# Sliding-window attention and two MoE layers: maxima over partitions on TensorE, lower halves and squares on GpSimd, a new instruction order

## The chip, the cores and the metric

The kernel runs on one core of a Trainium2 chip. The metric is the device time of one execution in microseconds (us), median of the runs; smaller is better. TensorE is called PE, VectorE DVE, ScalarE ACT, GpSimd POOL and SyncE, which issues the DMAs, SP.

## What is computed

The reference, cut to what matters (4 batches, 8 heads, 576 positions, head dimension 64, window 64; d_model 512, d_ff 1536):

```
scores = where(mask, scale * q @ k.T, -1e9);  attn = softmax(scores);  x = attn @ v     # x: 2304 tokens x 512
xn = x / sqrt(mean(x * x) + 1e-6) * rms_g
x = (silu(xn @ w_gate) * (xn @ w_val)) @ w_out                                      # first MoE layer
out = (sigmoid(x @ w_gate2) * (x @ w_val2)) @ w_out2                                # second
```

Weights arrive as float64, and the products are made as three products of f16 halves (upper by upper, upper by lower, lower by upper).

## The kernel before

The 2304 tokens are six blocks of 384. For each weight tile of the first layer (128 x 1024 values, tiles 0 to 11 alternately gate and value, 12 to 17 output) there are these steps: `w_load` (an SP DMA of 1 MB), `w_max` (maximum of the raw words on DVE, L244, then over the partitions on GpSimd, L247, then scales on DVE, L248, L249, L253, L255), `w_conv` (ACT L271, DVE L272 and L273: f64 words to f32), and `w_split` (upper half on ACT, L337, lower half on DVE, L339).

The attention works in pairs of pieces of 64 queries: `st_s` makes scores on PE (mask product L400, scores L406) and reduces them (L413 to L416, L418), ACT takes exponentials (L422), DVE sums and normalises (L423, L424, L431 or ACT L429); `st_tr` transposes on PE (L439), `st_pv` multiplies with the values (L476), copies (L478) and squares (ACT L481). `rms_first` takes the mean of the squares by a PE product (L519, L521), a power on GpSimd (L522), spreads the result over the partitions by PE (L527, L528) and scales x (L531); `split_first` makes its f16 halves (ACT L536, DVE L537). These must be done ahead of the first MoE product.

A gate unit of the first MoE layer is 12 products for the gate (`moe_g`, L576, into one of two PSUM banks, tag "gv"), ACT tanh L588, DVE L589, 12 products for the value (`moe_v`, L576 too), DVE L599, then the halves of h (`moe_h`, ACT L609 and DVE L610). There are 12 such units per block. The output product of a block is `moe_o` (L625 to L627). Blocks 2 to 5 and the second layer use other forms (L782, L893).

The order of instructions on every engine comes from one table of numbers, ORDER, which `arrange` turns into dependencies between neighbours of an engine. So a row of the order lists below stands where the table puts it, and engines meet only at their waits.

## Time and profile before

| | us |
|---|---|
| median of 3 runs (869.39, 869.86, 869.9) | 869.86 |
| profiled execution | 868.72 |
| its span | 866.9 |
| PE busy in the span | 844.9 |
| DVE busy | 728.7 |
| ACT busy | 552.8 |
| GpSimd busy | 36.5 |

The span is what the trace covers, from the first instruction to the end of the last output transfer; 1.8 us of the profiled execution lie outside. Its own time is 1.1 us under the median of the runs. Busy time is summed over instructions of an engine; the share alone doesn't say which one sets the end.

### The profile page before, as it was taken

To read this page: it belongs to the slowest core of one execution; us is meant where nothing else is said; L and a number is where in the kernel's file an instruction comes from. 1 tells how busy PE (TensorE), PEld (TensorE's weight loads), DVE (VectorE), ACT (ScalarE), POOL (GpSimd) and SP (SyncE) were. 2 spreads that over 40 slices of the span, in tenths; PEclk is the share of its full clock that TensorE was granted. 3 is DMA by queue.
4 is the path that set the end of the run, shared out by engine and by line. 5 is a ranking of instruction groups with operands and counts; after the bars stand their busy time and mean duration, and the time that the engine had idled before them with its cause. 6 is when DMAs were issued, how large, how long until landed. Compare 5 with 4: busy or idle time off the path is not lost.

```text
span 866.9 us, 15579 instructions
## 1 busy us (share of the span) xinstructions
PE 844.9 (97%) x6084; PEld 522.0 (60%) x6084; DVE 728.7 (84%) x1387; ACT 552.8 (64%) x1214; POOL 36.5 (4%) x46
## 2 busy tenths in 40 slices
PE   4799999999999999999999999999999999999998
PEld 3566666666666666666666666666666666666664
DVE  6999999989887796979789889999979859535695
ACT  5988878766568776355565567677557567235541
POOL 0100200100000100100000000000000000000000
PEclk8799999999999999999999999999999999999999
DMA  9764433121202035202412766446151112024034
GB/s 341 281 219 180 179 159 99 43 94 48 87 31 81 1 141 189 79 1 86 158 50 98 231 225 231 156 149 228 53 170 50 49 44 87 1 82 146 1 110 155
DMA packets 33193, 104.19 MB, mean 120 GB/s; under 512 B 3808, under 2 KB 11360, under 8 KB 27872
## 3 DMA queue, kind: packets, MB, share of 16 engines
q1 hardware_dynamic: 33120, 103.20, 34.0%
q8 instruction: 47, 0.77, 0.4%
q14 instruction: 26, 0.21, 0.1%
HBM read 82.35 MB, written 20.84 MB: 119 GB/s over the span
## 4 chain that ended last, share of the span: by engine, by line
PE 82%; DVE 12%; ACT 2%; DMA 2%; issue 1%; SPq 1%; POOL 0%; ACTq 0%; DVEq 0%
PE bank L782 46%; PE bank L893 14%; PE bank L576 5%; PE bank L625 4%; PE bank L626 4%; PE bank L627 4%; DVE wl L339 2%; DMA wl<-in_moe_w_gate_dram 2%; DVE wl L273 1%; PE bank L476 1%; PE bank L439 1%; PE bank L406 1%; ACT sm L422 1%; DVE th L599 1%; DVE wmax L244 1%
## 5 line engine op out<-in xcount | busy, mean ns | idle before, releaser
L782 PEld LDWEIGHTS <-wl 128*128 128x128 f16 x2520 | 245.9, 98 | 163.5 <-issue 1.5
L782 PE MATMUL bank<-att,wl 128*128 128x384 f16 x2016 | 338.1, 326 | 0.0
L893 PEld LDWEIGHTS <-wl 128*128 128x128 f16 x756 | 74.0, 98 | 48.9
L576 PE MATMUL bank<-xhl,wl 128*128 128x384 f16 x576 | 98.4, 326 | 0.1
L795 ACT ACTIVATE bank<-bank 128x384 f32<-128x384 f32 x120 | 56.5, 475 | 62.0 <-PE bank L782 31.9
L782 PE MATMUL bank<-xhl,wl 128*128 128x384 f16 x504 | 86.5, 326 | 0.2 <-ACT bank L795 0.2
L576 PEld LDWEIGHTS <-wl 128*128 128x128 f16 x576 | 55.5, 98 | 36.4 <-issue 0.7
L625 PE MATMUL bank<-wl,wl 128*128 128x384 f16 x192 | 62.7, 326 | 0.2
L627 PE MATMUL bank<-wl,wl 128*128 128x384 f16 x192 | 62.6, 326 | 0.0
L626 PE MATMUL bank<-wl,wl 128*128 128x384 f16 x192 | 62.6, 326 | 0.0
L337 ACT ACTIVATE wl<-wl,isc 128x1024 f16<-128x1024 f32 (+1 forms) x48 | 54.7, 1145 | 10.2 <-DVE wl L317 4.4
L893 PE MATMUL bank<-xhl,wl 128*128 128x384 f16 x264 | 51.7, 326 | 0.0
L244 DVE TENSOR_REDUCE wmax<-wl 128x1 f32<-128x1024 f32 x36 | 43.7, 1214 | 4.7 <-DMA wl<-in_moe_w_val_dram 2.6
L422 ACT ACTIVATE sm<-sm,nm 128x128 f32<-128x128 f32 x96 | 37.2, 389 | 14.3 <-DVE nm L416 14.0
L893 PE MATMUL bank<-wl 128*128 128x384 f16 x222 | 45.9, 326 | 0.0
L271 ACT ACTIVATE wl<-wl 128x1024 f32<-128x1024 f32 x36 | 41.6, 1154 | 6.7 <-DMA wl<-in_moe_w_out_dram 3.2
L429 ACT ACTIVATE sm<-sm,su 128x128 f32<-128x128 f32 x120 | 38.6, 391 | 7.6 <-DVE su L424 7.3
L339 DVE SCALAR_TENSOR_TENSOR wl<-wl,isc,wl 128x1024 f16<-128x1024 f32 (+1 forms) x32 | 38.4, 1199 | 3.0 <-ACT wl L337 3.0
L627 PEld LDWEIGHTS <-wl 128*128 128x128 f16 x288 | 28.2, 98 | 19.1 <-issue 0.4
L625 PEld LDWEIGHTS <-wl 128*128 128x128 f16 x288 | 28.2, 98 | 18.3 <-issue 0.9
L626 PEld LDWEIGHTS <-wl 128*128 128x128 f16 x288 | 28.2, 98 | 17.8 <-issue 0.6
L247 POOL PARTITION_ALL_REDUCE amax<-wmax x30 | 17.3, 594 | 436.4 <-DVE wmax L244 404.4
(387 smaller groups left out, 1461.0 us busy)
## 6 DMA issues: line engine op xcount, KB each, us to landing
wl<-in_moe_w_out_dram SPq DMA_DIRECT2D x15, 1024.0 KB, 5.3
wl<-in_moe_w_val_dram SPq DMA_DIRECT2D x13, 1024.0 KB, 5.8
wl<-in_moe_w_gate_dram SPq DMA_DIRECT2D x13, 1024.0 KB, 5.3
att<-f SPq DMA_DIRECT2D x28, 384.0 KB, 3.8
vn<-in_v_dram SPq DMA_DIRECT2D x27, 256.0 KB, 4.2
f<-xhl SPq DMA_DIRECT2D x14, 384.0 KB, 3.9
att<-in_k_dram SPq DMA_DIRECT2D x13, 384.0 KB, 3.3
xhl<-x SPq DMA_DIRECT2D x6, 768.0 KB, 7.2
```

The source lines that it names most:

```text
L244: V.tensor_reduce(out=r1[:, i:i + 1], in_=wraw(layer, j + i)[:, :, 1].bitcast(F32), axis=AX.X, op=ALU.max, apply_absolute_value=True)
L271: A.activation(out=y.bitcast(F32), in_=hi.bitcast(F32), func=AF.Prelu, scale=2.0 ** -112, alpha=-2.0 ** 32)
L337: A.activation(out=hi, in_=y, func=AF.Copy, scale=sc)
L339: V.scalar_tensor_tensor(out=lo, in0=y, scalar=sc, in1=hi, op0=ALU.mult, op1=ALU.subtract)
L422: A.activation(out=s[e][:, c], in_=pv[e][:, c, :] if st else s[e][:, c], func=AF.Exp, scale=scale if st else 1.0, bias=nm[:, j:j + 1], acc ...
L576: T.matmul(pb[:, 0:n], lhsT=w_, rhs=x_, start=(c == 0), stop=(c == m - 1))
L625: T.matmul(o[c][:, 0:n], lhsT=wh[:, cs], rhs=hi, start=st, stop=False)
L626: T.matmul(o[c][:, 0:n], lhsT=wh[:, cs], rhs=lo, start=False, stop=False)
L627: T.matmul(o[c][:, 0:n], lhsT=wl[:, cs], rhs=hi, start=False, stop=en)
L782: T.matmul(pb[:, 0:NMAX], lhsT=w_, rhs=x[:, t, kk], start=first and kk == n == 0, stop=kk == 1 and n == 2, skip_group_check=not first)
L795: A.activation(out=o[:, 0:NMAX], in_=i[:, 0:NMAX], func=AF.Copy)
L893: T.matmul(pb[:, 0:NMAX], lhsT=w_, rhs=x[:, t], start=st and s == ss[0] and n == 0, stop=s == ss[-1] and n == 2, skip_group_check=not st)
```

## The change

Three parts of the code change, and the table of the order is new.

- `all_max` is new. It replaces the maximum over partitions on GpSimd for the first twelve weight tiles (six pairs) and for the gains: a PE transpose into a PSUM bank (L239), a small DVE reduce (L241), and a second PE transpose which spreads the result over the partitions (L242). Seven sets of three instructions.
- GpSimd takes the halves of tiles 3, 5, 7, 9 and 11 (`POOL_LO`): it scales the tile in place (L349), ACT copies the upper half (L350), GpSimd subtracts for the lower one (L352). For the other tiles the lines are L354 (ACT) and L356 (DVE). It also takes the squares of the first two pieces (L499) and the lower halves of h of block 0 (L630).
- The maxima of the second pair of weight tiles (2 and 3) are taken with those of the first, in the attention's stages, and the second conversion uses them.

```diff
@@ -42,6 +42,7 @@
          (("W", 1, 2, 1), "17 s1")]
 PLAN2 = "W00 W01 W02 W10 P00 W11 W12 W20 P10 W21 W22 W23 P20 W24 W25 W03 P21 W04 W05 W13 W14 W15 P01 P11"
 WIDE = set()
+POOL_LO = {(0, j) for j in range(3, 12, 2)}
 NSLOT = 18
 PACKED = {(0, 12), (0, 13)}
 NORM_ACT = {(p, e) for p in range(3, 18) for e in range(2)}
@@ -233,6 +234,14 @@
         r = raw_place(layer, j)
         SY.dma_start(out=raw_home(layer, j)[:, r * 2048:r * 2048 + 4096].bitcast(I32), in_=wsrc(layer, j))

+    def all_max(x, n, tag):
+        pb = bank(tag)
+        T.matmul(pb[0:n, 0:P], lhsT=x, rhs=ident, start=True, stop=True, is_transpose=True)
+        y = small("top")
+        V.tensor_reduce(out=y[0:n], in_=pb[0:n, 0:P], axis=AX.X, op=ALU.max)
+        T.matmul(pb[:, P:P + n], lhsT=y[0:n].to_broadcast([n, P]), rhs=ident[0:n, 0:n], start=True, stop=True, is_transpose=True)
+        return pb[:, P:P + n]
+
     def w_max(layer, j, n=1):

         r1 = small("wmax", 2)
@@ -244,8 +253,12 @@
                 V.tensor_reduce(out=r1[:, i:i + 1], in_=wraw(layer, j + i)[:, :, 1].bitcast(F32), axis=AX.X, op=ALU.max, apply_absolute_value=True)
         js = slice(j, j + n)
         am, p_ = amax[:, layer, js], pw[:, layer, js]
-        G.partition_all_reduce(am, r1[:, 0:n], channels=P, reduce_op=RED.max)
-        V.tensor_scalar(out=am, in0=am, scalar1=2.0 ** -112, scalar2=1.875 * 2.0 ** -117, op0=ALU.mult, op1=ALU.max)
+        top = am
+        if layer == 0 and j < 12:
+            top = all_max(r1[:, 0:n], n, "any" if j < 4 else "oat")
+        else:
+            G.partition_all_reduce(am, r1[:, 0:n], channels=P, reduce_op=RED.max)
+        V.tensor_scalar(out=am, in0=top, scalar1=2.0 ** -112, scalar2=1.875 * 2.0 ** -117, op0=ALU.mult, op1=ALU.max)
         V.tensor_scalar(out=p_.bitcast(I32), in0=am.bitcast(I32), scalar1=3, scalar2=0x7F800000, op0=ALU.logical_shift_left, op1=ALU.bitwise_and)
         if layer == 0 and j >= 12:
             return
@@ -275,9 +288,7 @@
     def gam_scale():
         a = small("gam")
         V.tensor_reduce(out=a, in_=rg, axis=AX.X, op=ALU.max, apply_absolute_value=True)
-        b = small("gamr")
-        G.partition_all_reduce(b, a, channels=P, reduce_op=RED.max)
-        pow2(pgam, b, 2.0 ** -40)
+        pow2(pgam, all_max(a, 1, "any"), 2.0 ** -40)
         V.reciprocal(out=a, in_=pgam)
         V.tensor_scalar(out=cg, in0=rg, scalar1=a, scalar2=2.0 ** 9, op0=ALU.mult, op1=ALU.mult)

@@ -333,7 +344,13 @@
         if layer == 1:
             parts = [(x, d[:, 0:1024], d[:, 1792:2816]), (wraw(layer, j)[:, 0:768, 0].bitcast(F32), d[:, 1024:1792], d[:, 2816:3584])]
         for y, hi, lo in parts:
-            if half == 0:
+            if (layer, j) in POOL_LO:
+                if half == 0:
+                    G.tensor_scalar(out=y, in0=y, scalar1=sc, scalar2=None, op0=ALU.mult)
+                    A.activation(out=hi, in_=y, func=AF.Copy)
+                else:
+                    G.tensor_tensor(out=lo, in0=y, in1=hi, op=ALU.subtract)
+            elif half == 0:
                 A.activation(out=hi, in_=y, func=AF.Copy, scale=sc)
             else:
                 V.scalar_tensor_tensor(out=lo, in0=y, scalar=sc, in1=hi, op0=ALU.mult, op1=ALU.subtract)
@@ -478,7 +495,10 @@
         A.activation(out=x, in_=pb, func=AF.Copy)
         want_v(2 * p + 3)
         if blk < DEFER:
-            A.activation(out=sq_tile(blk, off // P), in_=x, func=AF.Square)
+            if p < 2:
+                G.tensor_tensor(out=sq_tile(blk, off // P), in0=x, in1=x, op=ALU.mult)
+            else:
+                A.activation(out=sq_tile(blk, off // P), in_=x, func=AF.Square)

     xhl = {}

@@ -607,7 +627,7 @@
         h = wl2[:, o:o + 2 * n].rearrange("p (t n) -> p t n", t=2)
         hh[blk, f] = h
         A.activation(out=h[:, 0, 0:n], in_=th[:, 0:n], func=AF.Copy)
-        V.tensor_tensor(out=h[:, 1, 0:n], in0=th[:, 0:n], in1=h[:, 0, 0:n], op=ALU.subtract)
+        (V if blk else G).tensor_tensor(out=h[:, 1, 0:n], in0=th[:, 0:n], in1=h[:, 0, 0:n], op=ALU.subtract)

     def moe_o(blk, f):
         n = BLOCKS[blk]
@@ -1055,11 +1075,14 @@
         V.memset(mhalf, -0.5)
         gam_scale()
         a0 = attn_stages(0, 2)
-        c0 = conv_pair(0, 0)
+        c0, c1 = conv_pair(0, 0), conv_pair(0, 2)
         raw_n = (NSLOT - raw_place(0, 0)) // 2
         r0 = rms_items(0)
         for i, (n, f) in enumerate(a0):
             at(-20 + 0.5 * i, n, f)
+            if n == ("s", 2):
+                at(-20 + 0.5 * i, *c0.pop(0))
+                at(-20 + 0.5 * i, *c1.pop(0))
             if n == ("p", PART // P - 1):
                 at(-19.99 + 0.5 * i, *r0.pop(0))
                 at(-19.98 + 0.5 * i, *r0.pop(0))
@@ -1077,7 +1100,7 @@

         more_loads(2)
         for s in range(1, NG):
-            lst = conv_pair(0, 2 * s) + [(("d", 0, 2 * s), lambda s=s: more_loads(2 * s + 2))]
+            lst = (c1 if s == 1 else conv_pair(0, 2 * s)) + [(("d", 0, 2 * s), lambda s=s: more_loads(2 * s + 2))]
             place(lst, pos["GV", 0, 0, 2 * s - 2], pos["GV", 0, 0, 2 * s], post)
         lst = []
         for j in range(12, 18):
@@ -1208,53 +1231,52 @@
 
 ENGINES = ["PE", "DVE", "Activation", "Pool", "SP"]
 ORDER = (
-    'c-nPW2|yFq*3O+fNk{@D5FqRz$gb?GEK)!PDkv_fRT1mbR^?UeTCGc;wTo3NZT+h
...
+    'c-nPW30M=?7S6qQCJPCW1dy=G4zel&uI!)%1@{%JZMF8(wpMHFr+uxq&uU+7pS7E
...
```

The new order in three places (DVE and PE around the first product, GpSimd, SP). In the order lists a line number is that of the kernel from which the row is, so DVE's L339 is L356 behind the change, L273 is L286, L244 is L253, L413 is L430, L589 is L609, L599 is L619, L537 is L557, and PE's L576 is L596. `x2` is two alike in a row.

GpSimd's first rows, up to the third h, before: L279 and L247 are maxima over partitions, L522 the power of the mean square.

```order
L279 ISA gamr_119<-gam_117 128x1
L247 ISA amax<-wmax_470 128x2
L247 ISA amax<-wmax_367 128x2
L522 ISA
L522 TENSOR_TENSOR ry_305<-ra_304,mhalf 128x2
L522 TENSOR_TENSOR ry_356<-ra_355,mhalf 128x1
L247 ISA
L247 ISA amax<-wmax_367 128x2
L247 ISA amax<-wmax_470 128x2
```

Behind the change, the same place, with squares ahead, then the two powers, and then tiles 3, 5 and the first h's:

```order
L499 TENSOR_TENSOR xhl_289<-wl_76 128x512 x2
L542 TENSOR_TENSOR ry_328<-ra_327,mhalf 128x2
L542 TENSOR_TENSOR ry_379<-ra_378,mhalf 128x1
L349 TENSOR_SCALAR wl_76<-wl_76,isc 128x1024
L352 TENSOR_TENSOR wl_75<-wl_76,wl_75 128x1024
L630 TENSOR_TENSOR wl_76<-th_527,wl_76 128x384
L630 TENSOR_TENSOR wl_76<-th_467,wl_76 128x384
L349 TENSOR_SCALAR wl_76<-wl_76,isc 128x1024
L630 TENSOR_TENSOR wl_76<-th_602,wl_76 128x384
L352 TENSOR_TENSOR wl_75<-wl_76,wl_75 128x1024
L349 TENSOR_SCALAR wl_76<-wl_76,isc 128x1024
L630 TENSOR_TENSOR wl_76<-th_467,wl_76 128x384
```

The L247 are gone here, and the halves stand in their stead.

DVE from the two lower halves of x (L537), which the first product waits for, on. Before:

```order
L537 TENSOR_TENSOR xhl_316<-wl_76,xhl_316 128x4x256
L537 TENSOR_TENSOR xhl_316<-wl_76,xhl_316 128x4x128
L413 TENSOR_REDUCE nm_145<-bank_163 128x4
L272 TENSOR_SCALAR wl_76<-wl_76 128x1024
L413 TENSOR_REDUCE nm_145<-bank_164 128x4
L339 SCALAR_TENSOR_TENSOR wl_75<-wl_76,isc,wl_75 128x1024
L418 TENSOR_SCALAR nm_145<-nm_145 128x8
L272 TENSOR_SCALAR wl_76<-wl_76 128x1024
L244 TENSOR_REDUCE wmax_470<-wl_76 128x1
L589 SCALAR_TENSOR_TENSOR th_452<-th_452,bank_200 128x384
```

Behind the change (L557 is the same step, th and bank name the gate units' buffers):

```order
L557 TENSOR_TENSOR xhl_339<-wl_76,xhl_339 128x4x256
L557 TENSOR_TENSOR xhl_339<-wl_76,xhl_339 128x4x128
L430 TENSOR_REDUCE nm_148<-bank_209 128x4
L356 SCALAR_TENSOR_TENSOR wl_75<-wl_76,isc,wl_75 128x1024
L286 SCALAR_TENSOR_TENSOR wl_76<-wl_75,wl_76 128x1024
L430 TENSOR_REDUCE nm_148<-bank_166 128x4
L435 TENSOR_SCALAR nm_148<-nm_148 128x8
L609 SCALAR_TENSOR_TENSOR th_467<-th_467,bank_167 128x384
L253 TENSOR_REDUCE wmax_251<-wl_76 128x1
L285 TENSOR_SCALAR wl_76<-wl_76 128x1024
L619 SCALAR_TENSOR_TENSOR th_467<-th_467,bank_203 128x384
L356 SCALAR_TENSOR_TENSOR wl_75<-wl_76,isc,wl_75 128x1024
```

The first unit's L609 stands behind one L356 and one L286 where L589 stood behind L339, two L272, and L244.

PE at the same place, the last scores and the first L576, before (`sm` are the exponentials, `ident` the identity, `vn` the values):

```order
L406 MATMUL bank_163<-att 64x128
L406 MATMUL bank_164<-att 64x128
L439 MATMUL bank_125<-ident,sm_408 128x128 x4
L439 MATMUL bank_213<-ident,sm_407 128x128 x4
L576 LDWEIGHTS wl_75
L576 MATMUL bank_200<-xhl_316,wl_75 128x384
```

Behind the change:

```order
L423 MATMUL bank_166<-att 64x128
L423 MATMUL bank_209<-att 64x128
L548 MATMUL bank_203<-xhl_289,wl_76 128x128
L456 MATMUL bank_119<-ident,sm_422 128x128 x4
L456 MATMUL bank_128<-ident,sm_423 128x128 x4
L493 MATMUL bank_129<-sm_422,vn_369 64x64 x4
L493 MATMUL bank_129<-sm_422,vn_371 64x64 x4
L493 MATMUL bank_129<-sm_423,vn_369 64x64 x4
L493 MATMUL bank_129<-sm_423,vn_371 64x64 x4
L596 LDWEIGHTS wl_75
L596 MATMUL bank_167<-xhl_339,wl_75 128x384
```

L548 (L528 before) and the four times four L493 (L476 before) now stand between the scores and the first product.

SP, the loads of weight and value tiles in the first 20 us. Before:

```order
L234 DMA wl_76<-in_moe_w_val_dram 128x2048
L362 DMA wl_76<-in_q_dram 128x512
L363 DMA wl_76<-in_k_dram 128x768
L234 DMA wl_76<-in_moe_w_gate_dram 128x2048
L1047 DMA ident<-const 128x128
L234 DMA wl_76<-in_moe_w_val_dram 128x2048
L234 DMA wl_76<-in_moe_w_gate_dram 128x2048
L372 DMA wl_76<-in_v_dram 128x512 x3
```

Behind the change, up to the fourth weight tile:

```order
L235 DMA wl_76<-in_moe_w_gate_dram 128x2048
L379 DMA wl_76<-in_q_dram 128x512
L389 DMA wl_76<-in_v_dram 128x512 x3
L235 DMA wl_76<-in_moe_w_val_dram 128x2048
L235 DMA wl_76<-in_moe_w_gate_dram 128x2048
L235 DMA wl_76<-in_moe_w_val_dram 128x2048
```

Three loads of values stand ahead of the second weight tile; they stood behind the fourth.

## Rows read from the trace of the kernel before

**Rows 1.** The page, first part: busy time, share of the span and instructions.

```profile
PE 844.9 (97%) x6084; PEld 522.0 (60%) x6084; DVE 728.7 (84%) x1387; ACT 552.8 (64%) x1214; POOL 36.5 (4%) x46
```

**Rows 2.** Windows: us; PE, PEld, DVE, ACT, POOL busy; granted clock; DMA share, GB/s.

```profile
7.00:17.00 10.00, 3.76 (x72) 2.68 (x68) 8.51 (x23) 8.25 (x37) 0.35 (x1) 0.82 1.00 405
...
27.00:37.00 10.00, 7.01 (x90) 5.62 (x85) 10.00 (x18) 10.00 (x27) 2.87 (x2) 0.84 0.78 294
37.00:43.00 6.00, 3.88 (x39) 2.77 (x40) 5.96 (x14) 5.75 (x12) 0.00 (x0) 0.50 0.64 253
43.00:50.00 7.00, 7.00 (x68) 4.74 (x67) 6.83 (x14) 4.93 (x13) 0.37 (x1) 0.93 0.74 257
50.00:105.00 55.00, 54.73 (x486) 36.02 (x488) 54.99 (x102) 48.98 (x116) 4.35 (x6) 1.00 0.48 174
```

**Rows 3.** Waits of PE between 44 and 862 us: total, times, longest.

```profile
PE bank L439 <- ACT sm L429: 0.4, 1, 0.4
...
PE bank L626 <- DVE th L838: 0.2, 1, 0.2
```

**Rows 4.** The chain in the first 46 us: start us, us, what.

```profile
7.34 13.05 DMA wl<-in_moe_w_gate_dram
20.41 1.22 DVE wmax L244
...
21.72 1.23 POOL amax L247
...
24.99 0.17 DVE isc L253
...
25.75 1.14 DVE wl L273
...
26.97 1.19 DVE wl L339
...
44.15 1.95 PE bank L576 x12
```

**Rows 5.** Timeline of PE, 37 to 49 us: start, us, line, in brackets idle before.

```profile
39.76 0.58 PE L400 MATMUL bank<-wl 128*128 128x512 bf16 x1 [2.12 <-DVE wl L531]
40.27 1.99 PE L406 MATMUL bank<-att 64*64 64x128 f32 x32
42.19 1.97 PE L439 MATMUL bank<-ident,sm 128*128 128x128 f32 x8
43.95 2.16 PE L576 MATMUL bank<-xhl,wl 128*128 128x384 f16 x12
46.04 1.15 PE L476 MATMUL bank<-sm,vn 128*64 128x64 f32 x32
```

**Rows 6.** Timeline of DVE just ahead of the first L576.

```profile
40.75 1.82 DVE L537 TENSOR_TENSOR xhl<-wl,xhl 128x1024 f16<-128x1024 f32 x2
```

**Rows 7.** The page, DMA issues: count, KB each, us to landing.

```profile
vn<-in_v_dram SPq DMA_DIRECT2D x27, 256.0 KB, 4.2
```

**Rows 8.** Groups of PE by form, 0 to 44 us: busy us, mean ns.

```profile
L519 PE MATMUL bank<-wl,xhl 128*128 128x1 f32 x24 | 3.0, 252 | 0.6 <-ACT xhl L481 0.6
```

**Rows 9.** Groups of DVE by form, 43 to 105 us.

```profile
L339 DVE SCALAR_TENSOR_TENSOR wl<-wl,isc,wl 128x1024 f16<-128x1024 f32 x9 | 11.6, 1285 | 0.0
...
L610 DVE TENSOR_TENSOR wl<-th,wl 128x384 f16<-128x384 f32 x9 | 5.1, 564 | 0.0
```

**Rows 10.** Timeline of POOL at 298 us.

```profile
298.28 2.60 POOL L509 PARTITION_ALL_REDUCE att<-att  x1 [11.71 <-ACT bank L795]
```

**Rows 11.** Timelines of DVE at 298 and at 349 to 352 us.

```profile
298.73 1.72 DVE L838 TENSOR_TENSOR xo<-xhl,xo 128x384 f16<-128x384 f32 x1 [0.22 <-ACT xo L837]
...
348.98 1.21 DVE L244 TENSOR_REDUCE wmax<-wl 128x1 f32<-128x1024 f32 x1
...
351.23 0.55 DVE L838 TENSOR_TENSOR wl<-th,wl 128x384 f16<-128x384 f32 x1
```

**Rows 12.** Timeline of DVE at the twelfth L599.

```profile
106.12 0.55 DVE L599 SCALAR_TENSOR_TENSOR th<-th,bank 128x384 f32<-128x384 f32 x1
```

More of the change, by code (lines that the diff above doesn't have):

```diff
@@ new lines @@
+    '8ZL#sPJy_k4M~u%i+Y%d!S;)gcxBL<l>sP#scug!2=P2mgo<_bzLlcD2OdhX+HM@YFeguEbnYsS?F((_6;HfQdmzTmhS9@)D==ZOF%UF#r6mn+vgO-s?V5%^'
+    '0TMe|v%e17*a3TdTWXVGxL}X%K^RnYDRq>bA%Q~Y3m|}YIzq;f@t|ldxc>}IM%ca4J(U4Jz-4=*%3cR_4!ekuMcqU&vrtDlWE6Wpc?ZK|?CcEDF<Z=#X@66b'
+    '=#rRQkp?L{Y1_w2V?<%h6JLEvEKR%A$*7p3tb=39`sFYPvIjeQwRmF5`h{ME1ZoLqtW!$rp@TlC($2$B8_?JrDtXrELpFFAoQyW33P~HIfg~kFm9w<L=Lta)'
+    'BkFvrV!9OFl!7LGYX~1!2|!4|x9<SxzkJ^VBDlwfov~HhnbfOUT-2C#bppNrRbc!5bmgAeZmiLuabmM4lRHV?)optb$GYk+%sw%ltnqbe8+J7oD|EWz#Qf>H'
@@ new lines @@
+    'y!3OK4Ob@)Z+0irb_g*pJOCjgXgwjK2|Yn(f;ZBn3??zj7=;W8V~h5`LPT9jz5?_Losil0b{~|o&Q`SVT7?OtkliWL+4m3-j=+_l0g3Tv@c9O??Soe#@U9On'
+    'CsYo&8%xQa@P_abUu4gW%vZ#pl>;p?4&9%C)FP<}Wc>O{2RJ_!6vbtnu>~-*8|M+)muanX@-blFBO6_sfHcTnJM&7|{lpUqSCaDO38sBv_C?)>*s2)altQfn'
+    'VXafjp#@r)^O79v<nHD2Zn+9!TY$Q3!@8PrCo#TD_Ry6PiiMz;^3wunbn2ATJ)z}t9C{<9*;RqtNoi1Zr`#Wu#N8VOG;;4IZG1i<8>Ja$EcY<FJp)Sj4%(qp'
+    '2_A&HtJQH=96Lsq#%UjnMH*5Lx+%wSEs(=bc}GM!mWOuNcL%|i5LOkVcR3N<5CYJ+pWN)*Nx4_4+=pq>rap64RN03WsBmYD8X}z^O#(F@t}cO60OZZ?EpAJ{'
@@ new lines @@
+    ';!5Ufgn549$G}V~*qX8}n>cXddXi7C*pk|Oj>6n{@Yt3|W4yw{uX5Ht;PbYCTduGbtOfsg7`Ddxfc5-Z%x8XV6@07u)lab48seB=u(@0LmE01C|5FsLPvatn'
+    'SLra1Yt6}xIbr1X8~<1WxixgiFa0l;O8M!<<r$2vD<U3XK=bLmu4+gNfM38V#{7t2tMbST2{$FMrT^mU@&eEDN)zTabKKK-C57M0ax$LV9P*e0b4xvsw|Tvc'
+    'r3T{{I|FW(^U%yS!@85@S212I0xU8G3?DWePRE$f&6sByzi$y>E9`M$Xw5Y*(t^cD-1clpMLzXeeE$NA2skXpYYwdl#>y*}jJ9gHFjuC4-yB)}k@-go=Hwl('
+    '*&JBYB@hT+?4kwSZk?@coHRlGb<{NO=Js^_=8rc&*gRM@i9<dB%wUIQLWHSs_Ww3*Vhb$$lNNv>djYp}14h726&^ow+g%HS0KZQfYNRZAkFDxl|KNWiEt{S'
```

81 lines of the change are left out of this document (34 added, 47 removed).

## The prediction

> **What bounds the kernel now.** I read the page's first line, then the stretches, the waits of TensorE (PE), the chain of the first 46 us, and last the groups of VectorE (DVE) and GpSimd (POOL). PE is busy 97% of the span, and the whole trace holds some 1.0 us of waits for PE between 44 us and the last matmul: four lines of which the longest is 0.4 us [rows 1, 3]. So after 44 us only PE's own work counts, unless something new makes PE wait. Before 44 us PE is far from full: 3.88 of 6 us in 37 to 43, 7.01 of 10 in 27 to 37, while DVE is full there (10.00 of 10, 5.96 of 6) [rows 2]. The chain shows why: the fourth weight tile lands at 20.39 (7.34 + 13.05), DVE takes its maximum (1.22), GpSimd its maximum over partitions (1.23), and after that the chain is DVE work, conversions and splits at 1.14 to 1.19 us each [rows 4].
>
> The first product of the first MoE layer (L576) starts at 43.95. It needs both L537, which end at 42.57 (40.75 + 1.82) [rows 5, 6]. PE itself came 1.4 us later still: behind the last wait for L531 at 39.76 it did a mask matmul, 32 score matmuls and 8 transposes, in a stretch whose granted clock is 0.50, that is 1.2 GHz [rows 2, 5].
>
> After 43 us a second bound lies close behind PE: DVE is busy 54.99 of the 55 us from 50 to 105 [rows 2]. PE does not wait there, but DVE has nothing to spare for work that goes slower.
>
> **Term 1, the earlier start.** Counted in the order lists up to the second L537 (L557 in the new numbering), DVE has one L339 instead of three, three L273 instead of four, four L244 instead of six, and three new small L241. By the durations of the chain, 2 x 1.19 + 1.14 + 2 x 1.22 = 6.0 us go, and three small ones come at 0.17 each (the price of L253), 0.5 us [rows 4]. So DVE has 5.5 us less to do, and could be done at 37.1. It won't all be had. The fourth tile's load stands in SP's new order behind three loads of values that stood behind it: 3 x 256 KB [rows 7]. At the 405 GB/s of the stretch 7 to 17 [rows 2] this is an estimated 1.9 us, so it lands near 22.3, and now four maxima, two PE transposes with a reduce between, and a scale lie between it and the second pair's conversion. I give 2.6 us back for this and have DVE done at 39.7. In the new order the scores stand ahead of PE's last L548, and behind it only transposes and the products with the values, which lie beside L551 and L557, so PE starts the first product when DVE is done: 43.95 - 39.7 = 4.25 us gained. Bounds: 3 us (the fourth tile later still) to 6.8 us (no new gap).
>
> Those products with the values (L476, at 46.04 in the trace, 1.15 us [rows 5]) then lie ahead of the first product in PE's idle time: another 1.1 us. PE's later work is otherwise the same in sum.
>
> **Term 2, the transposes.** Fourteen PE instructions are added. The six of the gains and of the first two pairs lie in the first 40 us, beside PE's idle time, and cost nothing; if that cover goes they cost as much as the other eight. These stand between the products of the gate. Small matmuls with f32 operands took 3.0 us for 24 (L519), 0.125 each [rows 8], so 1.0 us; with the change between f16 weights and f32 operands on top, I take 1.4. Bounds 0.8 and 2.0. What leaves GpSimd, L247, is on the path once, at 1.23 us [rows 4]; the pair of transposes with L241 between them takes its place there, and I take it to last as long.
>
> **Term 3, GpSimd's new work.** GpSimd gets five scalings in place and five subtractions of 128x1024, twelve subtractions of 128x384, and two squares of 128x512. The trace shows no such operation on GpSimd. From below: the same arithmetic on DVE, L339 at 1.285 and L610 at 0.564 [rows 9]. From above: the one GpSimd operation on whole tiles, L509, holds DVE's two-input operations for as long as it reads its 384 columns: L838 took 1.72 us beside it at 298.73 against 0.55 undisturbed, so that it could start only 1.6 us after L509 began (298.73 + 1.72 - 0.55 - 298.28) [rows 10, 11]. Per column that is some 4.2 ns, so 4.3 us for 1024 and 1.6 for 384.
>
> DVE is relieved in turn. From the second L537 at 42.57 to the twelfth L599, which ends the last of block 0's gate units at 106.7 [rows 12], DVE has about 64 us of work now and about 57 in the new order: three L339 fewer (3.8) and twelve L610 fewer (6.8) by [rows 9], less the two maxima and one conversion that now fall behind the start, and less the small reduces. PE's work over the same units is about 57 too: 24 groups of twelve products at 1.95 us [rows 4] are 46.8, and the attention pieces and transposes between them the rest. So the two engines are even, without any hold.
>
> A hold breaks that evenness. About a third of these 57 us are operations with two inputs from SBUF (six L356, some ten L286), which GpSimd can hold as it held L838. In the new order the first subtraction (tile 3, POOL L352) is released while DVE stands at L356 and L286, ahead of L609 of the first unit, and L609 frees the bank for PE's third group. There a hold goes straight through to PE, with the price of one subtraction. The second such place is tile 7; tile 5 and tile 9 meet reduces, which are not held (L244 beside L509 took 1.21 at 348.98, as elsewhere [rows 4, 11]), and cost little; tile 11 meets L432 and L433 late, where DVE has air. All holds together: about 2.8 us if a subtraction takes 1.5, of which I let PE feel a little over half: at tile 3 nothing is spare, later units have air (L610 is gone from DVE). I take 1.5 us for a 1024 subtraction, nearer the DVE rows because it is the same arithmetic on whole tiles and L509 is a custom operation that crosses partitions. Term 3 is then +1.5 us. Bounds: 0 (all hidden) and +8.
>
> The Trainium skill, SBUF — State Buffer, section "Who interferes with whom", says that a DVE instruction with two SBUF inputs contends with a GpSimd instruction that reads SBUF, as a lock for the whole instruction, and that reduces stay free. The trace agrees (1.72 against 0.55). The Trainium skill, GPSIMD Engine Reference, section 3.1, has an elementwise f32 operation of two inputs and 2048 columns at 4497 ns, about twice DVE; by it a subtraction of 1024 is an estimated 2.25 us, term 3 would be near +4 and the time near 870, and no run here shows that price.
>
> **Smaller terms.** The squares (two of 128x512 on GpSimd, for ACT) lie ahead of L519 of block 0: between half of an L339, 0.6, and half of 4.3, 2.15 us each, they are counted in term 1's bound of 3 us. The clock: the stretch 37 to 43 has 0.50 and 43 to 50 has 0.93, so full clock came back at about 44.0 (7 x 0.07 / 0.5 = 1.0 us of half clock) after PE had worked without a break from 39.76 [rows 2, 5]. If the first groups start earlier and the clock does not follow, they run at 1.2 GHz: up to 2.2 us (half of the 4.25). I take 0, since PE has scores, transposes and products just ahead of them. The new order in the later stages: PE hardly waits there now [rows 3], so a new order can lose by a wait and gain nothing; I take 0.
>
> **Sum.** 868.72 (the profiled execution) - 4.25 - 1.1 + 1.4 + 1.5 = 866.3. The profiled execution was 1.1 us under the median, so 867.4.
>
> **The rivals.**
> - *Even and hidden:* GpSimd's operations cost DVE nothing, as their holds fall on reduces. For it: 7 us less DVE work in the stretch. Against: the place of tile 3. With a good start (-4.3 - 1.1) and cheap transposes (+0.8), 865; with fewer gaps at the start, 864.
> - *Gain eaten:* a subtraction takes some 2.3 us, between the ends of term 3, all holds together 6, of which PE feels about 4: 868.72 - 5.35 + 1.4 + 4 = 868.8, so 869.9, no change.
> - *GpSimd holds DVE:* at 4.3 us for a subtraction, an assumed half of that for a scaling, and 1.6 for each h, GpSimd's work in the stretch is 5 x 4.3 + 5 x 2.15 + 12 x 1.6 = 51 of 60 us, and PE waits for DVE at each unit, some 8 us: 868.72 - 5.35 + 1.4 + 8 = 872.8, so 873.9, slower. It decides from a price of about 2.9 us upward, where PE feels 5.7 us. For it: the L838 row. Against: L509 is another kind of operation.
> - *No earlier start:* the squares or the fourth tile keep DVE waiting till 42: 869 to 870.
>
> **How the numbers follow.** The forecast (866 to 869) has 0.38, hidden 0.15, eaten 0.22, held 0.20, no earlier start 0.05. About 0.2% (1.7 us) is what a measurement of this kernel can tell from no change. Of the forecast three quarters lie below 868.1. Faster: 0.15 + 0.29 + 0.04 of the eaten = 0.48. Same: 0.09 + 0.15 + 0.05 = 0.29. Slower: 0.03 + 0.20 = 0.23. The range leaves out the best half of the hidden case and the upper half of the held one: 864 to 873.5; the forecast's own range is 865.5 to 869.
>
> **What would show it.** The first product (L596) starting near 39.7: term 1; its rival is a start after 42. POOL L352 with a mean near 1.5 us, and DVE's L356 and L286 beside it with durations above 1.3: term 3; a mean above 2.9 with waits of PE for DVE L609 or L619 between 42 and 105 us is the held case. Waits of PE after 105 us that before does not have would make the whole reckoning wrong, as would a granted clock under 1.00 after the first product.

## The result, and the profile after

The changed kernel takes 877.54 us (median of 4 runs, 874.41 to 878.35) against 869.88 for the kernel before in the same comparison (869.39 to 870.23): a ratio of 1.0082, 95% interval 1.0055 to 1.0108. It is 0.8% slower. The forecast was 867.4 with a range of 864 to 873.5. The profiled execution took 876.78 us with a span of 875.0, 8.1 more than before.

The page's first part, as [rows 1]:

```profile
PE 850.5 (97%) x6098; PEld 524.8 (60%) x6098; DVE 727.6 (83%) x1377; ACT 549.9 (63%) x1212; POOL 70.9 (8%) x63
```

PE is busy 5.6 us more than in [rows 1], but half of that lies ahead of the first product, beside idle time. From the first product to the end of the span PE is busy 820.2 us (817.5 before) and idle 11.9 (5.5 before). The windows show where it idles; columns as in [rows 2]:

```profile
27.00:37.00 10.00, 7.81 (x117) 6.27 (x107) 9.74 (x24) 8.21 (x27) 2.79 (x3) 0.83 0.23 77
37.00:43.00 6.00, 4.40 (x43) 3.96 (x44) 4.58 (x11) 4.56 (x9) 1.46 (x1) 0.51 0.18 72
43.00:50.00 7.00, 5.31 (x30) 2.95 (x30) 6.96 (x8) 3.23 (x8) 2.29 (x1) 0.93 0.57 206
50.00:105.00 55.00, 50.90 (x418) 32.26 (x416) 54.01 (x96) 46.71 (x109) 34.49 (x20) 1.00 0.59 217
```

From 43 to 105 us PE is idle for 1.69 + 4.10 = 5.8 us, where it was idle for 0.27 [rows 2]. DVE is almost as full as before (54.01 of 55), although GpSimd now does five L356 and ten lower halves of h (L630) of this stretch. In 37 to 43 DVE has gaps (4.58 of 6) where it had none, and the granted clock is half, as before.

The waits of PE from 42 us to the end (total, times, longest), as [rows 3]:

```profile
PE bank L596 <- DVE th L609: 2.7, 4, 1.7
PE bank L242 <- DVE top L241: 1.9, 3, 0.8
PE bank L802 <- DVE xhl L730: 0.6, 1, 0.6
PE bank L802 <- ACT xhl L664: 0.6, 1, 0.6
...
```

PE waits for L609 of the gate units, as the held case said, and also for the small reduce between a pair of transposes, and twice late. PE's timeline around the first product L596, as [rows 5]:

```profile
38.60 0.79 PE L548 MATMUL bank<-xhl,wl 128*128 128x128 f32 x2 [2.74 <-DVE wl L551]
39.18 1.91 PE L456 MATMUL bank<-ident,sm 128*128 128x128 f32 x8
41.02 1.98 PE L493 MATMUL bank<-sm,vn 128*64 128x64 f32 x32
42.93 4.58 PE L596 MATMUL bank<-xhl,wl 128*128 128x384 f16 x24
49.20 6.48 PE L596 MATMUL bank<-xhl,wl 128*128 128x384 f16 x36 [1.69 <-DVE th L609]
```

The first product starts at 42.93, 1.0 earlier than in [rows 5], where 4.25 were forecast. The third group waits 1.69 us for L609. What DVE did there:

```profile
35.81 1.92 DVE L286 SCALAR_TENSOR_TENSOR wl<-wl,wl 128x1024 int32<-128x1024 int32 x1
37.65 0.89 DVE L547 TENSOR_SCALAR xhl<-ident,ry 128x128 f32<-128x128 f32 x1
...
43.55 1.27 DVE L356 SCALAR_TENSOR_TENSOR wl<-wl,isc,wl 128x1024 f16<-128x1024 f32 x1
44.74 3.15 DVE L286 SCALAR_TENSOR_TENSOR wl<-wl,wl 128x1024 int32<-128x1024 int32 x1
...
48.60 0.55 DVE L609 SCALAR_TENSOR_TENSOR th<-th,bank 128x384 f32<-128x384 f32 x1
...
77.11 2.40 DVE L285 TENSOR_SCALAR wl<-wl 128x1024 int32<-128x1024 int32 x1
```

And GpSimd, on the same clock:

```profile
35.48 2.99 POOL L349 TENSOR_SCALAR wl<-wl,isc 128x1024 f32<-128x1024 f32 x1 [0.19 <-DVE isc L266]
44.52 2.29 POOL L352 TENSOR_TENSOR wl<-wl,wl 128x1024 f16<-128x1024 f32 x1 [6.05 <-ACT wl L350]
...
76.81 2.15 POOL L352 TENSOR_TENSOR wl<-wl,wl 128x1024 f16<-128x1024 f32 x1
```

L286 takes 1.22 us where GpSimd is idle (it does so in a run below), 3.15 beside the subtraction at 44.52, and 1.92 beside the scaling at 35.48. L285, with one input, took 2.40 beside the subtraction at 76.81 against 0.69 undisturbed. Neither PE nor DVE waits for a result of GpSimd anywhere between 42 and 112 us, so a late tile is not what costs there. GpSimd's groups (busy, mean ns, idle before):

```profile
L349 POOL TENSOR_SCALAR wl<-wl,isc 128x1024 f32<-128x1024 f32 x5 | 16.1, 3217 | 7.2 <-DVE isc L266 7.2
L630 POOL TENSOR_TENSOR wl<-th,wl 128x384 f16<-128x384 f32 x12 | 14.0, 1179 | 17.7 <-DVE wl L286 10.4 <-ACT wl L629 7.3
L352 POOL TENSOR_TENSOR wl<-wl,wl 128x1024 f16<-128x1024 f32 x5 | 10.9, 2180 | 6.5 <-ACT wl L350 6.5
```

A subtraction takes 2.18 us where 1.5 were assumed, and a scaling, taken for cheaper than a subtraction, 3.22.

### The profile page after: what moved, and what is told of

Same layout as the page of the kernel before. It is cut to its first block, busy times and chain, and to the rows that moved or that the text cites. A ratio compares the mean times of both kernels' runs of the same rounds, so it can differ in the third digit from the quotient of the medians.

```text
span 875.0 us, 15643 instructions
## 1 busy us (share of the span) xinstructions
PE 850.5 (97%) x6098; PEld 524.8 (60%) x6098; DVE 727.6 (83%) x1377; ACT 549.9 (63%) x1212; POOL 70.9 (8%) x63
## 4 chain that ended last, share of the span: by engine, by line
PE 76%; DVE 14%; ACT 5%; DMA 3%; issue 1%; SPq 0%; ACTq 0%; DVEq 0%
PE bank L802 43%; PE bank L913 14%; PE bank L596 6%; PE bank L645 3%; PE bank L647 2%; PE bank L646 2%; DVE wl L286 2%; PE bank L493 2%; PE bank L456 2%; DMA f<-xhl 1%; DVE xhl L730 1%; ACT sm L439 1%; PE bank L423 1%; DVE wl L356 1%; DMA x<-xhl 1%
## 5 line engine op out<-in xcount | busy, mean ns | idle before, releaser
L596 PE MATMUL bank<-xhl,wl 128*128 128x384 f16 x576 | 99.4, 327 | 2.9 <-DVE th L609 2.7
L596 PEld LDWEIGHTS <-wl 128*128 128x128 f16 x576 | 55.4, 98 | 40.3 <-issue 6.1
L354 ACT ACTIVATE wl<-wl,isc 128x1024 f16<-128x1024 f32 (+1 forms) x43 | 48.5, 1136 | 14.2 <-DVE isc L266 7.3
L253 DVE TENSOR_REDUCE wmax<-wl 128x1 f32<-128x1024 f32 x36 | 43.1, 1210 | 1.2 <-DMA wl<-in_moe_w_val_dram 1.0
L260 POOL PARTITION_ALL_REDUCE amax<-wmax x24 | 12.4, 533 | 351.6 <-DVE wmax L253 340.2
L286 DVE SCALAR_TENSOR_TENSOR wl<-wl,wl 128x1024 int32<-128x1024 int32 x28 | 36.6, 1313 | 1.8 <-ACT wl L284 1.7
```

Source lines behind the costliest of these rows:

```text
L253: V.tensor_reduce(out=r1[:, i:i + 1], in_=wraw(layer, j + i)[:, :, 1].bitcast(F32), axis=AX.X, op=ALU.max, apply_absolute_value=True)
L286: V.scalar_tensor_tensor(out=y if (layer, j) in PACKED else hi, in0=y, scalar=3, in1=lo, op0=ALU.logical_shift_left, op1=ALU.bitwise_or)
L354: A.activation(out=hi, in_=y, func=AF.Copy, scale=sc)
L596: T.matmul(pb[:, 0:n], lhsT=w_, rhs=x_, start=(c == 0), stop=(c == m - 1))
```

## The experiments

Two theories stood at first. *Held*: GpSimd's reads make DVE slower, DVE sets the pace from 43 to 105 us, and PE waits. *The order or the transposes*: what costs is that the work stands elsewhere, or that PE transposes and then waits for a reduce. Later a third came in, on the parts by themselves. A kernel that moves instructions between engines has its table of the order written anew, with every other instruction where it was, and the moved ones where their predecessors stood in time.

| kernel | median us | ratio to before, 95% | span | first product | from there to the end of the span |
|---|---|---|---|---|---|
| before | 869.9 | | 866.9 | 43.95 | 822.9 |
| changed | 877.54 | 1.0055 to 1.0108 | 875.0 | 42.93 | 832.1 |
| tiles_written | 870.46 | 1.0002 to 1.0021 | 868.2 | 40.52 | 827.7 |
| h_written | 874.91 | 1.0047 to 1.0081 | 872.1 | 41.56 | 830.5 |
| all_written | 871.09 | 1.0001 to 1.0021 | 869.0 | 40.99 | 828.0 |
| scale_8 | 878.12 | 1.0072 to 1.0107 | 877.0 | 42.66 | 834.3 |
| subtract_written | 876.11 | 1.0060 to 1.0093 | 871.4 | 43.61 | 827.8 |
| tiles_on_dve | 877.70 | 1.0073 to 1.0103 | 875.7 | 40.84 | 834.9 |
| own_maxima | 871.73 | 1.0015 to 1.0034 | 870.1 | 42.41 | 827.7 |
| pairs_on_gpsimd | 915.47 | 1.0501 to 1.0541 | 914.1 | 43.35 | 870.8 |
| pairs_and_tiles | 897.33 | 1.0299 to 1.0336 | 896.4 | 41.04 | 855.4 |
| tiles_alone | 903.03 | 1.0370 to 1.0401 | 900.7 | 45.12 | 855.6 |
| h_alone | 910.57 | 1.0456 to 1.0491 | 908.0 | 44.13 | 863.9 |
| squares_alone | 873.52 | 1.0032 to 1.0062 | 872.5 | 49.51 | 823.0 |
| maxima_alone | 871.22 | 1.0012 to 1.0031 | 868.6 | 45.12 | 823.5 |
| maxima_and_h | 870.88 | 1.0005 to 1.0024 | 869.1 | 45.41 | 823.7 |
| maxima_and_tiles | 882.19 | 1.0133 to 1.0166 | 878.9 | 47.39 | 831.5 |
| all_in_old_order | 883.80 | 1.0152 to 1.0186 | 881.8 | 50.35 | 831.4 |

Each ratio is to the kernel before in the same comparison, whose median was 869.5 to 870.0. The last three columns are of the one profiled execution of each kernel; the last is the difference of the two before it.

**Taking GpSimd's reads away.** Five kernels leave every instruction in its place in the order and change what GpSimd reads. GpSimd's work gets shorter with it (a write of zeros takes 0.95 us), and ACT scales where GpSimd doesn't. tiles_written has the first two edits below, scale_8 the first alone (the scaling), subtract_written the second alone (the subtraction becomes a write), h_written the third alone (block 0), all_written all three.

```diff
-                    G.tensor_scalar(out=y, in0=y, scalar1=sc, scalar2=None, op0=ALU.mult)
-                    A.activation(out=hi, in_=y, func=AF.Copy)
+                    G.tensor_scalar(out=y[:, 0:8], in0=y[:, 0:8], scalar1=1.0, scalar2=None, op0=ALU.mult)
+                    A.activation(out=hi, in_=y, func=AF.Copy, scale=sc)
-                    G.tensor_tensor(out=lo, in0=y, in1=hi, op=ALU.subtract)
+                    G.memset(lo, 0.0)
...
-        (V if blk else G).tensor_tensor(out=h[:, 1, 0:n], in0=th[:, 0:n], in1=h[:, 0, 0:n], op=ALU.subtract)
+        if blk:
+            V.tensor_tensor(out=h[:, 1, 0:n], in0=th[:, 0:n], in1=h[:, 0, 0:n], op=ALU.subtract)
+        else:
+            G.memset(h[:, 1, 0:n], 0.0)
```

> This kernel leaves out the lower halves of tiles 3, 5, 7, 9 and 11: GpSimd scales 8 columns instead of 1024 (L349) and fills the lower half with zeros instead of subtracting (L352), so it only writes. Orders of all engines, ACT's instructions, the transposes, the h and the squares are as in the changed kernel. Theory 'holds': the changed kernel lost its time because GpSimd's whole-tile reads hold DVE (about 2.5 us ahead of the first product, 6 us behind it by the excess lengths of DVE's instructions in its trace). Then L286 and L285 are back to 1.2 and 0.7 us, the first product starts near 41.3, and the time is 870 to 871.5. Rival 'order': the transposes and the new order lose the time whoever does the halves; then 875 to 878.

> Leaves out the twelve lower halves of h of block 0: GpSimd fills them with zeros and reads nothing; the rest is the changed kernel. Theory 'holds': the holds by L630 in the trace are 1.7 us in all and meet small instructions, so 876 to 877 (0.5 to 1.5 us less than the changed kernel). Rival 'queue': the h on GpSimd make its tiles late, and that is the loss; then 874 or less. Rival 'order': no difference, 877.5.

> Leaves out the scaling in place of the five tiles (8 columns of 1024 are multiplied by one; ACT scales on its way to the upper half); the subtractions L352 stay at full length on GpSimd, over an unscaled tile. Theory 'holds': only the scaling of tile 3 lies beside DVE's work that counts (1.7 us of excess at 36 to 38.5, ahead of the first product); the first product starts near 41.3 and the time is 875 to 876, as the subtractions hold DVE as before. Rival 'late tiles': what costs is that a scaling takes 3.2 us and delays the tile; then most of the loss goes and it is 871 to 873.

> Leaves out the five subtractions alone: GpSimd fills the lower halves of tiles 3 to 11 with zeros (0.95 us, writing only), while it still scales the whole tiles in place (3.2 us each) as in the changed kernel. Orders unchanged. Theory 'subtraction': the 7 us that tiles_written gave back are the holds by L352 at L286 and L285, and the scalings meet reduces or cost only phases in which PE waits for nothing; then 870 to 872. Rival 'both': the scalings hold DVE too (2.5 us of excess ahead of the first product); then 872.5 to 875.

> tiles_written and h_written together: GpSimd reads nothing but the two squares and the small powers, in the changed kernel's orders. Theory 'holds': 869 to 870.5, what is left above the forecast of 867.4 being the transposes with their waits and two new waits at 228 and 511 us. Rival 'order': 875 to 878.

With these ten long operations of GpSimd out, 7.1 of the 7.7 us are gone (870.46). DVE's timeline in tiles_written, at the places shown above:

```profile
35.18 1.22 DVE L286 SCALAR_TENSOR_TENSOR wl<-wl,wl 128x1024 int32<-128x1024 int32 x1
36.31 0.28 DVE L547 TENSOR_SCALAR xhl<-ident,ry 128x128 f32<-128x128 f32 x1
...
42.79 1.22 DVE L286 SCALAR_TENSOR_TENSOR wl<-wl,wl 128x1024 int32<-128x1024 int32 x1
...
44.73 0.55 DVE L609 SCALAR_TENSOR_TENSOR th<-th,bank 128x384 f32<-128x384 f32 x1
```

Both L286 are back at 1.22, and L609 begins 4.2 us after the first product instead of 5.7. PE's waits in the same kernel, 42 us to the end:

```profile
PE bank L802 <- DVE xhl L805: 0.9, 1, 0.9
PE bank L802 <- DVE xhl L730: 0.6, 1, 0.6
...
PE bank L596 <- DVE th L609: 0.5, 2, 0.3
```

The wait for L609 falls from 2.7 to 0.5, and that for L241 is gone: PE waited for the small reduce because DVE was behind. The late waits stay, so they belong to the order, not to the holds. The twelve h halves cost less (874.91, below the 876 to 877 expected, of which 1.6 us lie behind the first product), and on top of the tiles nothing (871.09).

Neither edit by itself recovers the time, and both kernels are slower than either expectation. scale_8 is no faster than the changed kernel. Behind its first product it takes 834.3 us, so there the subtractions alone cost as much as both. Ahead of it L286 and L547 are back at 1.22 and 0.28, but the first product still comes at 42.66, since DVE waited 2.2 us for PE's L539 at 28 us (0.7 in the changed kernel). subtract_written gains 1.4 us in the median, and the two intervals overlap. Its profiled execution, the fastest of its four (873.30), gains 4.3 us behind the first product but begins it at 43.61. DVE there, and GpSimd's write:

```profile
36.32 1.93 DVE L286 SCALAR_TENSOR_TENSOR wl<-wl,wl 128x1024 int32<-128x1024 int32 x1
38.18 1.80 DVE L547 TENSOR_SCALAR xhl<-ident,ry 128x128 f32<-128x128 f32 x1
38.37 1.60 DVE L551 SCALAR_TENSOR_TENSOR wl<-wl,cg,bank 128x256 f32<-128x256 f32 x1
38.95 0.94 POOL L352 MEMSET wl<- 128x1024 f16 x1
```

The scaling ends at 38.99 and holds L286 as in the changed kernel. L547 and L551 are held longer than there (1.80 and 1.60 against 0.89 and 0.70), until the write of zeros ends, which has nothing to wait for and follows the scaling at once. So a GpSimd operation that only writes can hold DVE too. In tiles_written it does so once more (L285 at 72.33 takes 1.17 beside a write), so that kernel's gain, if anything, understates the holds. Why the two edits bring so much less singly than together is not shown further.

**The tiles' halves back on DVE.** `POOL_LO = set()`, each half placed where GpSimd began it.

> All twelve lower halves by DVE again (L356, 1.19 us each, placed in DVE's order where GpSimd had begun its subtraction); no scaling in place; h and squares stay on GpSimd, the transposes stay, nothing is left out. Theory 'hold': 5 x 1.19 us of DVE's own work take the place of 6.4 us of holds, but the work is at a known place and the five L350 no longer wait for a scaling; 871 to 874. Rival 'DVE even': DVE and PE are even in this stretch, so 6 us more on DVE are felt in full and it is 876 to 878, the same as the changed kernel.

It starts early, at 40.84, and takes 834.9 from there: as slow as the changed kernel. So in this stretch five L356 on DVE (5 x 1.28 = 6.4 us) cost what GpSimd's holds cost, and an early start is lost again when DVE sets the pace behind it. That DVE sets it is seen from the stretch between the end of the last L557 (L537 before) and the end of the twelfth L619 (L599 before), from the windows of each trace:

| kernel | stretch, us | length | DVE busy | PE busy |
|---|---|---|---|---|
| before | 42.57 to 106.67 | 64.1 | 63.9 | 63.8 |
| tiles_written | 41.08 to 104.12 | 63.0 | 61.0 | 61.4 |
| changed | 43.03 to 111.05 | 68.0 | 66.8 | 62.2 |
| tiles_on_dve | 41.42 to 110.49 | 69.1 | 67.1 | 61.7 |

In the three kernels with the new order PE's work is nearly the same, and the length goes with DVE's busy time.

**The transposes.** own_maxima is tiles_written with `V.tensor_copy(out=top, in_=r1[:, 0:n])` in place of `all_max` for the last four pairs.

> On top of tiles_written (GpSimd only writes the lower halves of tiles 3 to 11): the last four pairs of tiles leave out the maximum over partitions too, and take each partition's own maximum by a DVE copy of two columns into the same PSUM bank in place of PE transpose, DVE reduce and PE transpose. Orders and banks otherwise as in tiles_written. Theory 'transposes': the eight transposes last 1.2 us and the steps between f16 products and f32 transposes about 0.7 more, so 868 to 869 against 870.46 of tiles_written. Rival 'order': what tiles_written lost behind its first product belongs to the new order, and the transposes only take places where PE had air; 870 to 870.6.

Without these eight transposes the kernel is not faster than with them (871.73 against 870.46), so they are not what costs the 7.7 us. Their own price is smaller than what executions differ by: from the first product on PE is busy 818.3 us without them and 819.5 with them, 1.2 us more, while a wait of 1.9 us for a DMA came into the one profile without them.

**Putting the maxima back on GpSimd**, for the last four pairs; pairs_and_tiles has the tiles' halves on DVE too:

```diff
-            top = all_max(r1[:, 0:n], n, "any" if j < 4 else "oat")
+            if j < 4:
+                top = all_max(r1[:, 0:n], n, "any")
+            else:
+                G.partition_all_reduce(am, r1[:, 0:n], channels=P, reduce_op=RED.max)
+                top = bank("oat")[:, P:P + n]
+                V.tensor_copy(out=top, in_=am)
```

> The maxima over partitions of the last four pairs of tiles go by GpSimd again (L247's form, then a DVE copy of two columns into the same bank, so that the banks stay as they are); the first two pairs and the gains stay on PE; the rest is the changed kernel, nothing is left out. Theory 'transposes': the eight transposes cost 1.2 us and their waits for DVE's L241 1.9 us, so 874 to 875. Rival 'late DVE': those waits are DVE's lateness and come back at the next L609; then 876 to 877.5.

> pairs_on_gpsimd and tiles_on_dve together, nothing left out: what is left of the change is the earlier start (first two pairs of maxima by PE), squares and h on GpSimd, and the new order. Theory 'hold': 869 to 871. Rival 'DVE even': 874 to 876.

915.47 and 897.33: 38 and 20 us more than the changed kernel, whose whole loss is 7.7. Neither theory explains that; the third, below, does.

**Each part alone, in the order of before:** tiles_alone and h_alone have GpSimd's halves (the lines of the diff on L349 to L352, and on L630), squares_alone the two squares.

> The kernel before with one part of the change: the halves of tiles 3, 5, 7, 9 and 11 by GpSimd (scaling ahead of ACT's upper half, subtraction where DVE had its L339), every other instruction in the order of before. Theory 'hold': DVE has 6 us less of its own and 4 to 6 us of holds, and the maxima over partitions stand in GpSimd's queue behind 3 us scalings, so pairs come late: 871 to 876. Rival 'relief': DVE gains as much as it is held, PE waits for nothing in before, 869 to 870.5.

> The kernel before with the twelve lower halves of h of block 0 on GpSimd at the places where DVE had them; nothing else changed. DVE has 5.6 us less, holds are 2 us at most by the changed kernel's trace. Theory 'hold': PE waits for nothing from 44 us on in before, so the relief buys nothing and the holds are absorbed: 869.3 to 870.5. Rival 'queue': the maxima over partitions stand behind h in GpSimd's queue and come late: 871 or more.

> The kernel before with the first two squares of block 0 on GpSimd (1.45 us each by the changed kernel's trace, 0.5 on ACT); nothing else changed. Theory: the mean square (L519) waited for ACT by 0.6 us in before and now waits longer for GpSimd, but ACT is 1 us ahead behind it; the first product moves by -0.3 to +0.8 us: 869.5 to 870.8. Rival 'start': ACT was what the start waited for, and the first product comes 1 us earlier: 868.7 to 869.

tiles_alone and squares_alone took longer than either expectation, and h_alone far longer than its first (its rival, the queue, had only a lower bound). squares_alone loses its 4 us ahead of the first product, which comes 5.6 us later, since PE waits 4.0 us for the squares; from there it takes 823.0, as before. The tiles' halves alone cost 33 us, and the halves of h alone 41. GpSimd's timeline in h_alone says why:

```profile
54.98 0.36 POOL L247 PARTITION_ALL_REDUCE amax<-wmax  x1 [10.22 <-DVE wmax L244]
63.12 0.90 POOL L610 TENSOR_TENSOR wl<-th,wl 128x384 f16<-128x384 f32 x1 [7.79 <-issue]
70.11 0.73 POOL L247 PARTITION_ALL_REDUCE amax<-wmax  x1 [6.09 <-DVE wl L272]
80.19 1.78 POOL L610 TENSOR_TENSOR wl<-th,wl 128x384 f16<-128x384 f32 x2 [9.35 <-issue]
```

In these rows, when a subtraction follows a partition maximum, GpSimd stands idle for 7.8 and 9.4 us (6.7 at a third such place, 103.77), waiting for nothing that the profile shows. The kernel before has the same idle time already, in both directions, at places where PE waits for nothing:

```profile
89.42 1.13 POOL L522 TENSOR_TENSOR ry<-ra,mhalf 128x2 f32<-128x2 f32 x1 [7.30 <-issue]
...
104.65 1.77 POOL L247 PARTITION_ALL_REDUCE amax<-wmax  x2 [7.14 <-issue]
```

In h_alone DVE stands behind GpSimd's maxima, and PE behind DVE; PE's longest group of waits there:

```profile
PE bank L576 <- DVE th L589: 23.7, 4, 9.8
```

This was the third theory: the three parts only work together, since the transposes take the maxima off GpSimd, so that between 20 and 112 us nothing but elementwise work is left there. The last four kernels try it in the order of before. They have `all_max` for the twelve tiles (not for the gains, and with the second pair's maxima where they were); maxima_and_h has `(V if blk or f > 7 else G)` for h, maxima_and_tiles the `POOL_LO` lines, all_in_old_order both and the squares.

> Before's kernel, in before's order, with one part of the change: the maxima of the twelve weight tiles over the partitions go by PE transposes (fourteen minus the two of the gains: twelve). The gains' maximum stays on GpSimd. Theory A, that GpSimd's idle time of 7 to 9 us at each change between a partition maximum and an elementwise operation is what made the parts cost so much alone: nothing on PE waited for it in before, so this part alone brings no gain; 0.6 to 1.2 us of transposes on PE and up to 1 us of waits for the small reduce on a full DVE give 870 to 872, and between 22 and 95 us GpSimd shows no idle time put down to issue. Rival B, that the maxima on PE are a gain in themselves: 867 or less. Rival C, that they are what makes the changed kernel slow: 874 or more.

> The kernel maxima_alone, and the lower halves of h of units 0 to 7 on GpSimd instead of DVE, placed where DVE had them (units 8 to 11 stay on DVE, since the maxima of the output tiles on GpSimd follow at 105 us). Theory A: with no partition maximum between them the h halves cost no change of operation; DVE is relieved of 8 times 0.56 = 4.5 us and held for 8 times some 0.2: 869 to 872, beside the 910.6 of the twelve halves alone. Rival: the h halves themselves, not the changes, cost the 41 us; then 890 or more.

> The kernel maxima_alone, and the halves of tiles 3, 5, 7, 9 and 11 on GpSimd, scaled there in place, placed where ACT and DVE had them. Theory A: no change of operation between 35 and 95 us, so not the 903.0 of these halves alone; what is left is the hold of DVE, 5 subtractions of 2.2 us and 5 scalings of 3.2 us against 5 operations of 1.29 us taken from DVE: 872 to 877. Rival, that the halves themselves cost the 33 us: 890 or more.

> All three parts in the order of before: maxima of the twelve tiles on PE, five tiles' halves, eight of the twelve lower halves of h and the first two squares on GpSimd; the gains' maximum and four h halves stay where they were, and the maxima of the second pair keep their place. If the new order is what costs in the changed kernel (its late waits for L730 and L664 and a stretch of 4 us more between first product and last matmul than before even without any read by GpSimd): 873 or less, under the changed kernel. If the holds on DVE are all of it: 876 to 880, as the changed kernel or worse, since this order was not made for them. Waits of PE after 105 us should be as in before, under 1.1 us in sum.

maxima_and_h takes 870.88 where h_alone took 910.57 (with twelve halves instead of eight). Its GpSimd at the same place:

```profile
56.61 2.01 POOL L625 TENSOR_TENSOR wl<-th,wl 128x384 f16<-128x384 f32 x1 [19.62 <-DVE tg L270]
63.76 0.92 POOL L625 TENSOR_TENSOR wl<-th,wl 128x384 f16<-128x384 f32 x1 [5.14 <-ACT wl L624]
...
107.44 1.34 POOL L262 PARTITION_ALL_REDUCE amax<-wmax  x2 [7.57 <-issue]
```

It waits for its data, not for issue, until the first maximum of an output tile at 107.44, where PE doesn't wait for it. So the third theory held. The maxima on PE cost little (maxima_alone is 1.7 us over before in the median, and 0.6 from first product to end), and eight h halves on GpSimd next to nothing beyond that (+0.2 from first product to end).

Against maxima_alone, where DVE makes them, the tiles' halves on GpSimd add 8.0 us from first product to end: maxima_and_tiles took 882.19, above the 872 to 877 expected, though far below the 903.03 of tiles_alone. ACT's waits in it, 42 to 112 us, show one reason:

```profile
ACT wl L355 <- POOL wl L354: 7.0, 3, 2.6
```

ACT's copy waits there for GpSimd's scaling (L354, L349 in the changed kernel), and with it all that stands behind it on ACT; the changed kernel, whose order starts the scalings earlier, has 0.7 us of this.

all_in_old_order, where 873 or 876 to 880 were expected, took 883.80, 6.3 us more than the changed kernel. Both of its expectations failed, and it does not show that the old order suits the holds worse: from the first product to the end it takes 831.4 us and the changed kernel 832.1, and the first product comes at 50.35 instead of 42.93. The difference is in the opening. PE waits 3.0 us there for the squares, and DVE, in both last kernels, 2.2 us for the second power of the mean square, because the first scaling was given a place between the two powers here.

No kernel here beats the one before. The nearest, tiles_written, leaves five lower halves out; the nearest that leaves nothing out is maxima_and_h (a ratio of 1.0014).

## Why the prediction was wrong, point by point

**What bounds the kernel** was right: behind 44 us PE, and DVE close behind it. "Unless something new makes PE wait" is what came.

**Term 1, the earlier start (-4.25 forecast, -1.0 had).** This step failed first. The sum counted DVE's work up to L557, and the order did take it away. Without GpSimd's scaling the first product comes at 40.5 to 41.0 in four kernels, near the forecast of 39.7, and at 42.4 and 42.7 in two (own_maxima, scale_8), which were 1.3 and 2.8 us behind tiles_written already when DVE read the first mean square (L541, near 26 us). What was missing is that the first scaling (L349, 35.48) runs beside the last DVE work ahead of the product. It held L286 by 0.70 and L547 by 0.61 us against the same rows of tiles_written. The squares were thought of here, the scaling was not. The rest of the difference is within what openings differ by.

A larger error stands behind it: an earlier start was counted as a gain of the whole kernel. DVE work that stood ahead of the first product, two lower halves among it, went behind it, where DVE was just as full [rows 2]. tiles_written, in which DVE is free of all five halves, starts 3.4 us earlier than before and needs 4.8 more from there (2.0 of them busy time of PE, the rest waits); tiles_on_dve starts 3.1 us earlier and needs 12.0 more.

**The products with the values (-1.1).** They do stand ahead of the first product, at half the full granted clock (0.51 in 37 to 43 us, so 1.98 us). Whether it brought anything can't be told: DVE's last L557 ends at the same moment.

**Term 2, the transposes (+1.4).** This came out about right. PE has 2.0 us of them behind the start in its rows, and from the first product on its busy time grows by 1.2 with them, both from before to maxima_alone and from own_maxima to tiles_written. The working was low (0.125 us each was the busy time of L519 divided by its count, while the rows of the transposes have 0.21 and 0.27), and the allowance for the change of operands made up for it. The wait for L241 of 1.9 us was not in the sum, but it is DVE's lateness: it goes when the holds go, and is there in tiles_on_dve.

**Term 3, GpSimd's new work (+1.5 forecast, 4.4 had).** This is the other step that failed. The mechanism was forecast as it came, at the place that was named: the first subtraction, beside L286, ahead of L609, through to PE's third group. The size was not. A subtraction takes 2.18 us where 1.5 were taken as "nearer the DVE rows"; the estimate from the Trainium skill, GPSIMD Engine Reference, section 3.1, of 2.25 us was within 0.1. In the prediction's own working that price stood only as a rival. The scaling, put at half a subtraction in the held rival and at nothing in the sum, takes 3.22. And the holds were priced for instructions with two inputs, with reduces as the only other neighbours, while L285 with its single input is held too: 2.40 against 0.69. The Trainium skill, SBUF — State Buffer, section "Who interferes with whom", lists `tensor_scalar` among the operations that can take the shared ports; this trace agrees, and the prediction had used only the line on two inputs. Added up over DVE's instructions from 42 to 112 us that took longer than the same instruction does elsewhere, some 6 us lie beside L352. PE felt 4.4 (832.1 against 827.7 in tiles_written), three times the sum's 1.5, and besides this there is what the first scaling cost ahead of the product.

**The evenness of DVE and PE.** Both engines' work up to the twelfth unit was put at 57 us. In tiles_written, where GpSimd spares DVE the five halves and hardly holds it, DVE is busy 61.0 us and PE 61.4 of the 63.0. They are even, as was said, but at 61, so there was no slack for a hold. For PE [rows 2] had said so: it was busy 54.73 of 55 us in the old order. The holds then raised DVE to 66.8, and the stretch to 68.0.

**The smaller terms.** The later stages, taken at 0, missed two waits of 0.6 us (L730, L664) that come with the new order: the one on L730 is there, at 0.6 us, in tiles_written, subtract_written and tiles_on_dve too, while others of up to 0.9 us come and go between executions. maxima_alone, in the old order, has none of them. New waits after 105 us were what the prediction itself had named as a sign against its whole reckoning.

**The rivals.** *Held* had the direction, the place and, at 873.9, the nearest time, but its condition was wrong: it was to decide from a price of 2.9 us for a subtraction upward, and the price is 2.2. *Gain eaten* had that price to within some 0.1 and 4 us felt, and ended at 869.9 because it kept the early start.

**What stays open.** The changed order, with the tile halves on DVE, is 6.8 us slower than the old order with them there (877.70 against 870.88; they differ also in four h halves, the squares and the gains' maximum). In the profiles it starts 4.6 us earlier and needs 11.2 more from there, of which 9.9 are idle time of PE, most of it waits for DVE in block 0's units (L609 3.8, L241 1.8, L253 0.7) and the late waits. Which moves in the table make DVE late there is not shown. With the tile halves on GpSimd the two orders need the same from the first product on (832.1 and 831.5), and the new one opens earlier. Of PE's 5.6 us of added busy time all fourteen transposes are 3.4 by their groups; the rest lies in several groups at slightly longer means, some of it at half clock, and is not explained here.
